# Attention and soft mixture of experts: x turned by transposing transfers, one exponential tile in every step on VectorE

## Chip, cores, metric

One core of a Trainium2 chip. The metric is the device time of one execution in microseconds (us). Most executions of a kernel agree within 0.3%; a run 1.5% above the fastest of its kernel counts as slow and is left out of ratios.

## The reference

```python
# q, k, v: (8, 12, 448, 64); phi: (768, 32); w1: (8, 768, 1024); w2: (8, 1024, 768)
scores = cap * np.tanh((q @ k.T) / 8 / cap)            # cap = 30
attn = softmax(scores); x = (attn @ v)                 # -> x: (3584, 768)
logits = x @ phi
d = softmax over tokens of logits; slot_input = d.T @ x
slot_out = relu(slot_input @ w1) @ w2                  # per expert
out = softmax over slots of logits @ slot_out
```

The attention output x is needed twice: as it is, for `slot_input`, and with its columns on the partitions, for `logits`. Turning x is what the change is about.

## The kernel before

The loop has 56 steps, seven to a batch of 12 heads (six pairs). In a step ScalarE takes the tanh and the exponential of six tiles of 448 columns. `aux` holds side jobs by step and slot; a step runs its slots in the order "a", "b", the rest of the product with V with its norm, "c", "d". In these traces each engine starts its instructions in program order.

One tile of a step can be taken by VectorE, as five operations, here in five of seven steps:

```python
    PARTS = {0: ((0, "a", (0, 1)), (0, "d", (2, 3)), (1, "a", (4,))),
             ...                       # the same for 1, 2, 3 and 6
    def poly_exp(j, ops):
        t = exs[j][:, 0, :]
        steps = (
            lambda: dve.tensor_scalar(xe, t, ...),                        # to an integer
            lambda: dve.tensor_scalar(xb.bitcast(U16), whole, 7, None, ALU.logical_shift_left),
            lambda: dve.scalar_tensor_tensor(xp, frac, p2, frac, ALU.add, ALU.mult),
            lambda: dve.scalar_tensor_tensor(xp, xp, p1, frac, ALU.add, ALU.mult),
            lambda: dve.scalar_tensor_tensor(t, xp, p0, xb, ALU.add, ALU.mult))
```

The norm, the turning of x and the logits:

```python
    def norm(pr, s0, s1, pv):
        ...
        dve.reciprocal(rec, pv[:, 0:s1 - s0, DH:W])
        dve.tensor_tensor(xq[Q][:, h, s0:s1, :], pv[:, 0:s1 - s0, 0:DH], rec..., op=ALU.mult)

    def x_transp(pr):
        ps = psT.tile([P, S], BF16, name="xps", tag="T")      # tag "T": one PSUM buffer
        turn_x(ps, 0, pr, range(NG))                          # TensorE transposes
        t = xs.tile([P, S], BF16, name="xT", tag="xT", bufs=2)
        dve.tensor_copy(t, ps)
        xTs[pr] = t

    def logits(Q, ps=None):
        ps = psT.tile([P, NG, NS], F32, name="lps", tag="T")
        ...                                                   # matmuls phib x xT, two pairs
        dve.tensor_copy(lgs[b], ps)                           # or an add
```

The loads of q, k and of all weights cast from f32 and are issued by GpSimd (the software queue); v comes plain, issued by SP. GpSimd also casts v.

The softmax here doesn't subtract the row's maximum and nothing guards it: scores larger than these inputs give would overflow.

## Time and profile before

| | before |
|---|---|
| time | 311.0 us (median of four) |
| span of the profiled run, mean clock of TensorE | 312.0 us, 0.987 |
| a batch, by the distance of norms | 31.6 us |
| landing of v / q / k, median | 5.1 / 8.4 / 6.9 us |

### The profile page before, as it was taken

The page shows a single profiled execution, that of the slowest core. Times are in us where ns is not written, and L with a number is a line of the kernel's source. Part 1 is how long each engine was busy: PE and PEld are TensorE (multiplying, and loading weights), DVE is VectorE, ACT ScalarE, POOL GpSimd, SP SyncE. Part 2 cuts the span into 40 slices and gives each one's busy share as a digit, 9 for nine tenths or more (in the row PEclk, how much of TensorE's full clock was granted, in tenths as well). Part 3 has the DMA queues.
Part 4 walks back from the last instruction along what each step waited for, and adds up shares of the span by engine and source line. Part 5 has one row for each costly group of instructions (what it writes and reads, how often), then busy time and mean ns, then how long its engine had stood idle before and what let it go on. Part 6 is the DMA issues. An engine that isn't in the chain of part 4 may idle for free.

```text
span 312.0 us, 11360 instructions
## 1 busy us (share of the span) xinstructions
PE 272.0 (87%) x5069; PEld 191.5 (61%) x5069; DVE 212.9 (68%) x463; ACT 271.9 (87%) x209; POOL 135.8 (44%) x176
## 2 busy tenths in 40 slices
PE   8999889998999988988899889888998899998820
PEld 6666666676667766666676667666766677642400
DVE  2533589958995899589958995799578944236840
ACT  3899999999999999999999999999999997126730
POOL 4192836393639345924492549155913350000000
PEclk9999999999999999999999999999999999999995
DMA  7979999999999999999899999999999548948997
GB/s 262 188 140 204 196 185 181 205 192 200 208 218 185 192 219 200 204 202 223 157 178 211 207 217 182 195 220 223 179 204 205 115 159 313 352 155 298 391 410 313
DMA packets 57488, 67.75 MB, mean 217 GB/s; under 512 B 3808, under 2 KB 53600, under 8 KB 57440
## 3 DMA queue, kind: packets, MB, share of 16 engines
q0 software_dynamic: 42448, 35.31, 73.6%
q1 hardware_dynamic: 14704, 31.50, 29.4%
q8 instruction: 39, 0.64, 0.8%
q10 hardware_dynamic: 288, 0.23, 0.2%
q14 instruction: 9, 0.07, 0.1%
HBM read 91.32 MB, written 18.87 MB: 353 GB/s over the span
## 4 chain that ended last, share of the span: by engine, by line
PE 46%; DVE 40%; ACT 8%; issue 2%; DMA 1%; DVEq 0%; ACTq 0%
PE pv L353 11%; DVE xq L361 7%; PE sc L295 7%; PE junk L595 6%; DVE work L333 5%; DVE work L334 5%; DVE ex L335 5%; DVE work L332 4%; ACT ex L304 3%; ACT ex L308 3%; DVE work L330 3%; DVE kT L265 3%; DVE qT L265 2%; DVE xT L410 2%; PE kps L263 2%; PE pv L381 2%
## 5 line engine op out<-in xcount | busy, mean ns | idle before, releaser
L304 ACT ACTIVATE ex<-sc 128x1344 bf16<-128x1344 f32 (+1 forms) x113 | 152.1, 1510 | 3.8 <-PE sc L295 3.7
L308 ACT ACTIVATE ex<-ex 128x2240 bf16<-128x2240 bf16 (+4 forms) x58 | 137.1, 2368 | 0.1
L353 PE MATMUL pv<-vbd,ex 128*128 128x130 bf16 (+1 forms) x1610 | 94.3, 211 | 13.8 <-DVE xq L361 11.5
L353 PEld LDWEIGHTS <-ex 128*128 128x128 bf16 (+1 forms) x1680 | 75.9, 101 | 34.2 <-DVE xq L361 9.6
L295 PE MATMUL sc<-qT,kT 64*64 64x448 bf16 x672 | 74.0, 364 | 2.2 <-DVE qT L265 1.3
L273 POOL CAST vbd<-vraw 64x896 bf16<-64x896 f32 x23 | 21.4, 929 | 83.6 <-PE pv L353 73.5
L447 POOL COPY e<-E 128x512 bf16<-128x512 bf16 x9 | 6.4, 715 | 64.9 <-ACT E L441 30.8
L410 DVE COPY xT<-xps 128x448 bf16<-128x448 bf16 x47 | 18.2, 388 | 23.8 <-PE xps L404 23.4
L361 DVE TENSOR_TENSOR xq<-pv,rec 128x448 bf16<-128x448 f32 x46 | 28.7, 624 | 1.6
L295 PEld LDWEIGHTS <-kT 64*64 64x64 bf16 x672 | 24.9, 106 | 7.0 <-issue 4.9
L333 DVE SCALAR_TENSOR_TENSOR work<-work 128x448 f32<-128x448 uint16 x35 | 26.6, 761 | 0.0
L595 PEld LDWEIGHTS <-ones 128*128 128x128 bf16 x326 | 20.5, 105 | 8.1 <-issue 5.2
L334 DVE SCALAR_TENSOR_TENSOR work<-work 128x448 f32<-128x448 f32 x35 | 24.4, 697 | 1.2
L110 POOL DMA_DIRECT2D w1b<-in_moe_w_dram x32 | 24.7, 773 | 0.0
L274 POOL CAST vbd<-vraw 64x896 bf16<-64x896 f32 x23 | 23.3, 1014 | 1.4
L381 PE MATMUL pv<-ones 128*128 128x57 bf16 x620 | 23.9, 188 | 0.0
L595 PE MATMUL junk<-ones 128*128 128x128 bf16 x283 | 21.5, 225 | 1.2 <-DVE xq L361 1.0
L335 DVE SCALAR_TENSOR_TENSOR ex<-work 128x448 bf16<-128x448 f32 x35 | 21.9, 626 | 0.2
L265 DVE COPY kT<-kps 128x896 bf16<-128x896 bf16 x23 | 14.3, 621 | 11.1 <-PE kps L263 9.7
L381 PEld LDWEIGHTS <-ones 128*128 128x128 bf16 x620 | 20.7, 96 | 0.3
L265 DVE COPY qT<-qps 128x896 bf16<-128x896 bf16 x23 | 14.2, 618 | 5.8 <-PE qps L263 5.8
L182 POOL DMA_DIRECT2D qb<-in_q_dram x22 | 16.4, 745 | 3.8 <-DMA kraw<-in_k_dram 3.8
(117 smaller groups left out, 343.1 us busy)
## 6 DMA issues: line engine op xcount, KB each, us to landing
w1b<-in_moe_w_dram POOLq DMA_DIRECT2D x32, 384.0 KB, 8.7
vraw<-in_v_dram SPq DMA_DIRECT2D x23, 448.0 KB, 5.1
w2d<-in_moe_w_dram POOLq DMA_DIRECT2D x20, 384.0 KB, 8.6
w2t<-w2d SPq DMA_DIRECT2D x20, 384.0 KB, 5.7
out_dram<-ob SPq DMA_DIRECT2D x8, 768.0 KB, 6.8
qb<-in_q_dram POOLq DMA_DIRECT2D x22, 224.0 KB, 8.4
kb<-in_k_dram POOLq DMA_DIRECT2D x22, 224.0 KB, 6.9
w2b<-in_moe_w_dram POOLq DMA_DIRECT2D x12, 384.0 KB, 8.3
```

Source lines behind the costliest of these rows:

```text
L110: pool.dma_start(out=w1b[e][:, js, fs], in_=w1r[:, e, js, fs])
L265: dve.tensor_copy(t, ps)
L295: pe.matmul(sc[cs, u, 0:S], qkT["k", Q][r, c, cs], qkT["q", Q][r, :, cs], start=True, stop=True)
L304: act.activation(exs[j][:, half * CS + u0:half * CS + u1, :], sc[:, u0:u1, 0:S], ACT.Tanh, scale=qk_scale / cap)
L308: act.activation(exs[j][:, u0:u1, :], exs[j][:, u0:u1, :], ACT.Exp, scale=cap)
L333: lambda: dve.scalar_tensor_tensor(xp, frac, p2, frac, ALU.add, ALU.mult),
L334: lambda: dve.scalar_tensor_tensor(xp, xp, p1, frac, ALU.add, ALU.mult),
L335: lambda: dve.scalar_tensor_tensor(t, xp, p0, xb, ALU.add, ALU.mult))
L353: pe.matmul(out_, exs[j][r, u, q0:q0 + (HP if tail else P)], v_, start=(c == 0 and g == gs[0] < NF), stop=(c == NT - 1), skip_group_check= ...
L361: dve.tensor_tensor(xq[Q][:, h, s0:s1, :], pv[:, 0:s1 - s0, 0:DH], rec.to_broadcast([P, s1 - s0, DH]), op=ALU.mult)
L381: pe.matmul(home, ones, ones[:, 0:512 - NT * W], start=False, stop=True, skip_group_check=True)
L595: pe.matmul(junk if home is None else home, ones, ones, start=True, stop=True)
```

## The change

Its intent: free TensorE of turning x and VectorE of copying the turned x, by letting a transposing transfer do it, and use the time that VectorE gets to take an exponential tile in all seven steps. The five operations of a tile are spread over the step so that no norm or copy waits long. x moves into one long buffer `xall` of eight slots; its column groups are reordered so that one transfer of 128 x 512 serves a pair; the odd group of 64 is covered by two small matmuls with `phi2`.

```diff
-    PARTS = {0: ((0, "a", (0, 1)), (0, "d", (2, 3)), (1, "a", (4,))),  ... 1, 2, 3, 6 alike
+    PARTS = {0: ((0, "<b", (0,)), (0, "c", (1, 2, 3)), (0, ">d", (4,))),
+             1: ((0, "a", (0,)), (0, "r", (1,)), (0, "c", (2, 3)), (0, ">d", (4,))),
+             ...
+             5: ((0, "<d", (0,)), (1, "<b", (1,)), (1, ">b", (2,)), (1, "c", (3,)), (1, ">d", (4,))),
+             6: ((0, "a", (0,)), (0, ">b", (1,)), (0, ">d", (2,)), (1, "<b", (3, 4)))}
@@ norm: slot "r" lies between the reciprocal and the multiplication
+        for f, a in between:
+            f(*a)
@@ x_transp
+        if pr < NDX:                                   # all but the last four pairs
+            x0 = pr % 8 * S
+            t = xs.tile([P, NG, P], BF16, name="xT", tag="xT", bufs=3)
+            sp.dma_start_transpose(out=t, in_=xall[:, x0:x0 + HP + S])
+            xTs[pr] = t
+            return
@@ phi_mms, the tail of 64
+            for m in range(2):
+                for n, ph in enumerate((phi2, phib)):
+                    pe.matmul(dst[m * HP:m * HP + HP], t[HP:P, 0, n * HP:n * HP + HP], ...)
@@ fillers (dependence-free matmuls): 106 per batch before, 82 after; places of the jobs
-            at(j + 4 + k, "a", x_transp, p + k)
+            at(*((j + 3 + k, "c") if p + k < NDX else (j + 4 + k, "a")), x_transp, p + k)
... (cut: start of the kernel, tile sizes, the end part's slots)
```

## The prediction

> **What bounds the kernel now.** The work up to about 257 us is a loop of 56 steps: ScalarE (ACT) takes two tanh of 1344 columns and one exponential of 2688 columns per step, TensorE (PE) makes scores and the product with V, VectorE (DVE) copies, norms, and in five of each seven steps takes one 448-column tile of the exponential as a polynomial of five instructions. Seven steps are one batch.
>
> I read the chain of work that ended last first, from the page:
>
> ```profile
> PE 46%; DVE 40%; ACT 8%; issue 2%; DMA 1%; DVEq 0%; ACTq 0%
> ```
>
> ACT is 8% of it, though the page has ACT at nine tenths or more in the slices of the loop. The stretches by engine, of two batches in the middle, say how full each engine is:
>
> ```profile
> 99.30:130.93 31.63, 28.93 (x592) 21.09 (x591) 25.38 (x56) 31.63 (x24) 18.63 (x23) 1.00 1.16 202
> 130.93:162.59 31.66, 28.50 (x584) 20.78 (x585) 25.67 (x55) 31.66 (x24) 17.00 (x23) 1.00 1.12 185
> ```
>
> (Columns: length, PE, PE weight load, DVE, ACT, POOL, clock, DMA share, GB/s.) A batch takes 31.63 us; ACT has no idle time, PE 2.7 us, DVE 6.25 us. The timeline of ACT tells the two apart, by the starts:
>
> ```profile
> 98.38 2.76 ACT L304 ACTIVATE ex<-sc 128x1344 bf16<-128x1344 f32 x2
> ...
> 103.05 2.78 ACT L304 ACTIVATE ex<-sc 128x1344 bf16<-128x1344 f32 x2
> ...
> 107.35 2.80 ACT L304 ACTIVATE ex<-sc 128x1344 bf16<-128x1344 f32 x2
> ...
> 129.42 2.89 ACT L304 ACTIVATE ex<-sc 128x1344 bf16<-128x1344 f32 x2
> ```
>
> A step in which ACT does all six tiles is 103.05 - 98.38 = 4.67 us, one in which DVE takes a tile 107.35 - 103.05 = 4.30 us, so a tile is worth 0.37 us. Seven steps of ACT are 5 x 4.30 + 2 x 4.67 + 0.20 (a small exponential) = 31.04 us, just 129.42 - 98.38. But the loop of PE and DVE needs 31.63 us: the norm, in the chain in order of time,
>
> ```profile
> 106.96 0.62 DVE xq L361
> ...
> 111.29 0.64 DVE xq L361
> ...
> 138.59 0.62 DVE xq L361
> ```
>
> comes again after 138.59 - 106.96 = 31.63 us. So PE, which starts with a lead, loses about 0.6 us of it to ACT per batch, and late in the loop ACT waits:
>
> ```profile
> 241.27 1.30 ACT L304 ACTIVATE ex<-sc 128x1344 bf16<-128x1344 f32 x1
> 242.98 1.29 ACT L304 ACTIVATE ex<-sc 128x1344 bf16<-128x1344 f32 x1 [0.41 <-PE sc L295]
> ```
>
> 1.71 us between these two starts instead of the usual 1.17 (a pair without a wait takes 2.34, as from 98.38 to 100.72 us). All such excess of the starts from 170 us on I sum to about 2.0 us. So **ACT and the PE-DVE loop bind together**, 31.04 and 31.63 us per batch. Inside the loop DVE has no idle between 103.07 and 123.7 us (the five steps with a polynomial); in the other two steps PE has none, filler matmuls included.
>
> The third thing is DMA, from the DMA view of the same batch (99.3 to 131 us):
>
> ```profile
> q0 software_dynamic: 5259, 4.94, 100.5%
> q1 hardware_dynamic: 823, 1.39, 14.5%
> ```
>
> The casting loads write 4.94 MB and, being f32 at the source, read 9.88 MB; with v's 1.39 MB that is 11.3 MB in 31.63 us, 356 GB/s. The best slice of the page is 410 GB/s, so the engines are about 87% full.
>
> **What the Trainium skill says.** "DMA: Bandwidth & Descriptors", section "DMA Transpose (X-bar)": the plain transposing transfer is issued from SP or ACT, takes 2-byte types and writes SBUF; only two such streams at once are unsafe. Here all go from SP. No transfer of this trace transposes, so its speed isn't shown. The same page, "Anatomy of one DMA", puts about 2.0 us of fixed time on a transfer on the software path; the trace agrees for the hardware path too in that the smallest stores (192 KB) land in a median of 2.1 us. Its section "Issuing engines are not separate DMA queues" has all queues on the same 16 engines: the trace agrees, v's 448 KB take 5.1 us beside the software queue. "VectorE: DVE Perf Modes", "The three transpose paths", gives 1309 ns for a 128x128 by DMA against 390 ns on PE; here PE records 219 ns each, three pipelined in 0.33 us.
>
> **The change part by part, per batch.**
>
> ACT: two more tiles go to DVE, 31.04 - 2 x 0.37 = 30.3 us. In the whole loop 48 tiles instead of 35: 13 x 0.37 = 4.8 us less.
>
> DVE loses six copies of x (L410) and gains two polynomials. The groups give their means:
>
> ```profile
> L410 DVE COPY xT<-xps 128x448 bf16<-128x448 bf16 x47 | 18.2, 388 | 23.8 <-PE xps L404 23.4
> ...
> L333 DVE SCALAR_TENSOR_TENSOR work<-work 128x448 f32<-128x448 uint16 x35 | 26.6, 761 | 0.0
> ...
> L334 DVE SCALAR_TENSOR_TENSOR work<-work 128x448 f32<-128x448 f32 x35 | 24.4, 697 | 1.2
> ```
>
> A polynomial is 398 + 421 + 761 + 697 + 626 = 2903 ns by the means, about 2.6 us by the distance of starts where nothing disturbs it. A copy is 0.39 us, 0.31 by starts. So 25.4 + 2 x 2.75 - 6 x 0.33 = 28.9 us. Part of the mean is a disturbance: an L334 at 108.27 takes 1.25 us instead of 0.62 while POOL casts v. With a polynomial in every step all three casts of a batch can meet one, say 0.3 us more: **29.2 us of 30.3, 96%**. That is why the operations are spread, one even between the reciprocal and the multiplication.
>
> PE loses six times three 128-wide and two 64-wide transposes, about 0.42 us each set as they issue (108.84 to 109.15 us and the matmuls they hold up), 2.4 us; gains six times two small matmuls for the tail, some 0.3 us; and the fillers go from 106 to 82, about 1 us. 28.9 - 3.1 = 25.8 us: it no longer binds in any step, and the wait of DVE for the transposes (23.4 us in the whole run) goes.
>
> DMA: six transposes of 128 x 512 x 2 B = 131 KB, 0.79 MB. Then (11.3 + 0.79) MB in 30.3 us = 399 GB/s, **97% of the best slice**, if a transpose moves as fast as a copy. Each has from the end of its norm to the logits of its pair: now 107.6 to 111.0 us, 3.4 us, at the shortest. Estimate for landing: between the 2.1 us of the smallest store and v's 5.1 us, some 3 us, since it has less than a third of v's bytes. It hides, with little to spare; PE can wait another microsecond, as the scores are that far ahead of ACT.
>
> Start and end: three pairs of fillers fall out of the first transposes, at most 0.3 us. The last four pairs keep the old way, so from 257 us all shifts as it is.
>
> The sum, if ACT alone binds: 4.8 us of tiles + 2.0 us of late waits + 0.1 = 6.9 us, 311.0 - 6.9 = 304.1 us. I don't expect all of it. DVE at 96%, in order, will wait here and there for PE, and what it waits it can't get back. If DVE and PE turn at 30.8 us per batch instead of 30.3, that is 7 x 0.5 = 3.5 us, of which the lead PE starts with hides about 1.5: 2.0 us lost, **306 us**.
>
> **The rivals.** First, *DVE becomes the bound*: for it speak the 96% and the full DVE between 103 and 124 us; against it that DVE's long waits were for the x transposes that go, and that the order was plainly arranged with care. At 31.2 us per batch: 7 x 0.9 - 1.5 = 4.8 lost, 309 us. Second, *DMA becomes the bound or lands late*: for it the 97% and a transpose slower than a copy; against it that the weights leave some slack outside full batches. With transposes at half the speed of a copy the demand is 12.9 MB, 31.4 us at 410 GB/s, late q or k loads would stall PE, 309 to 311 us; if each logits waited 1.5 us more for a transpose, 3 x 7 x 1.5 us, even a third of it kept gives over 315. Third, *ACT keeps the pace*: 304 us. For it the three microseconds that PE gets per batch.
>
> **Range and chances.** ACT's pace 35% (304), a partly lost pace 45% (about 306.5), DVE or DMA as the bound 16% (309 to 311), late transposes 4% (over 315). 2% faster is under 304.7, which only the first can give, and not all of its cases. Predicted 306.0 us, range 303.5 to 310.0; faster 0.27, same 0.69, slower 0.04.
>
> **What would show it.** In the profile after: starts of ACT 4.30 us apart in all steps; the batch by the norm (now 31.63 us) at 30.3 to 31.0; DVE in a middle batch 28.5 to 29.5 us busy; PE some 26; x transposes landing in about 3 us, with no wait of PE for them of weight; DMA share higher; the part after the loop unchanged within 0.5 us. A median landing over 5 us, waits of the logits' matmuls for the transfers, DVE without idle time with ACT waiting for scores, or a loop that ends no earlier would make the prediction wrong.

## More of the kernel before

The lines that carry the argument stand in the prediction. A few more are wanted for comparison. The page's clock row, one digit per fortieth of the span, in tenths of full speed:

```profile
PEclk9999999999999999999999999999999999999995
```

and from the list of waits (engine, line, what it waited for: us in total, times, longest), the only wait of ScalarE in the loop:

```profile
ACT ex L304 <- PE sc L295: 3.7, 5, 2.0
```

The clock is at 90% or more until the last slice, and ScalarE nearly never waits for scores. The DMA view's issues have the two landing times from which the prediction estimates that of a transpose, v's and the smallest store's, and between them q's (KB each, median us from issue to landing):

```profile
vraw<-in_v_dram SPq DMA_DIRECT2D x23, 448.0 KB, 5.1
...
qb<-in_q_dram POOLq DMA_DIRECT2D x22, 224.0 KB, 8.4
...
out_dram<-obh SPq DMA_DIRECT2D x20, 192.0 KB, 2.1
```

## The result

| | before | after |
|---|---|---|
| time, median (lowest to highest) | 311.0 us | 363.1 us (360.3 to 367.7) |
| ratio after/before | | 1.164, 95% interval 1.155 to 1.173 |
| span, mean clock | 312.0 us, 0.987 | 360.0 us, 0.893 |
| time at half clock inside the loop | 0 | 68 us |
| from the norm of pair 45 of 48 to the end | 51.8 us | 52.45 us |
| landing of v / q / k, median | 5.1 / 8.4 / 6.9 us | 6.5 / 9.5 / 7.1 us |

The time at half clock is counted up to the norm of pair 45; the texts below say 61 us, which leaves out its last stretch, 6.8 us from 282.7 us on. A ratio is the mean time of one kernel's fast runs over the mean of the other's in the same rounds, so it isn't quite the ratio of the medians in the table. The change is slower by 16%. All of it lies in the loop. The page's chain of work that ended last, by engine and then by line, now reads:

```profile
PE 41%; DMA 27%; DVE 23%; ACT 4%; issue 2%; DVEq 0%; SPq 0%; ACTq 0%
DMA xT<-xall 25%; PE pv L360 14%; PE sc L300 6%; DVE xall L369 5%; PE kps L260 4%; DVE work L340 3%; DVE work L341 3%; DVE work L339 3%; PE junk L621 2%; DVE ex L342 2%; DVE work L337 2%; ACT ex L309 2%; PE so_ps L794 2%; PE pv L388 2%; PE hp L766 2%
```

DMA was 1% of this chain and is 27%; 25% are the transposing transfers alone. The tile view of the turned x has their time from issue to landing, and the list of waits has who paid:

```profile
DMA to landing us min/median/max: 2.4/7.0/11.8
```

```profile
PEld L430 <- DMA xT<-xall: 44.1, 21, 5.5
ACT ex L309 <- PE sc L300: 42.5, 30, 5.7
PE lps L430 <- DMA xT<-xall: 37.7, 16, 5.4
```

L430 are the logits. The profile keeps weight loads (PEld) and matmuls (PE) of TensorE on two tracks, and both wait for the same transfers here, so 44.1 and 37.7 us are largely the same time and are not added. TensorE stands, the next scores come late, and ScalarE, which waited 3.7 us before, waits 42.5 us. One such wait, in the chain in order of time (start, length, what):

```profile
115.52 0.64 DVE xall L369
116.21 8.01 DMA xT<-xall
124.27 0.32 PE lps L430 x5
...
138.54 0.54 DVE xall L369
139.13 7.04 DMA xT<-xall
```

and the same place in the timeline of TensorE, where the bracket is the idle time before:

```profile
116.30 0.85 PE L360 MATMUL pv<-vbd,ex 128*128 128x130 bf16 x12 [0.23 <-DVE xall L369]
...
124.27 0.32 PE L430 MATMUL lps<-phib,xT 128*128 128x32 bf16 x5 [4.89 <-DMA xT<-xall]
...
124.84 1.50 PE L360 MATMUL pv<-vbd,ex 128*128 128x130 bf16 x12
```

The norm ends at 116.2 us; the transfer lands 8 us later; TensorE stands 4.89 us of these. The same twelve matmuls then take 1.50 instead of 0.85 us, because the clock has been halved (granted clock 0.50 from 124.84 to 126.34 us). The page's clock row shows how often that happens:

```profile
PEclk9999888998999789688885997996999799999995
```

What the change was for does come where nothing disturbs it. The timeline of ScalarE:

```profile
101.10 2.45 ACT L309 ACTIVATE ex<-sc 128x1344 bf16<-128x1344 f32 x2
...
105.40 2.48 ACT L309 ACTIVATE ex<-sc 128x1344 bf16<-128x1344 f32 x2
...
127.58 1.29 ACT L309 ACTIVATE ex<-sc 128x1344 bf16<-128x1344 f32 x1 [4.17 <-PE sc L300]
```

4.30 us from step to step at first, then 4.17 us of waiting. The stretches by engine, of two middle batches (length, PE, weight load, DVE, ACT, POOL, clock, DMA share, GB/s):

```profile
104.46:142.00 37.54, 28.80 (x547) 20.95 (x547) 29.33 (x61) 30.89 (x23) 17.84 (x23) 0.91 1.29 187
142.00:180.00 38.00, 31.84 (x510) 22.49 (x509) 27.55 (x58) 30.61 (x23) 16.43 (x22) 0.78 1.14 180
```

No engine is full: 37.5 us for 30.9 us of ScalarE.

A side finding, about the result and not the time. The timeline of VectorE shows the first operation of two tiles (L337) before the second operation (L339) of either:

```profile
106.92 0.38 DVE L337 TENSOR_SCALAR work<-ex 128x448 int32<-128x448 bf16 x1
...
108.45 0.38 DVE L337 TENSOR_SCALAR work<-ex 128x448 int32<-128x448 bf16 x1
108.86 0.43 DVE L339 TENSOR_SCALAR work<-work 128x448 uint16<-128x448 uint16 x1
```

In `PARTS`, residue 5 starts its tile in slot "<d" and goes on in the next step's "<b", after residue 6 has overwritten the shared `work` in "a". By the code and by the order in this trace that tile gets its neighbour's exponential. The comparison with the reference passes all the same, as it does when x isn't turned at all (run 6), so it is blind to both. The kernel after is thus not right as it stands, nor is any run below with these places; it is an error to mend in any use of them.

### The profile page after: what moved, and what is told of

Its sections match the earlier page's. It is cut to its first block, busy times and chain, and to the rows that moved or that the text cites.

```text
span 360.0 us, 10935 instructions
## 1 busy us (share of the span) xinstructions
PE 280.0 (78%) x4764; PEld 196.2 (55%) x4764; DVE 234.2 (65%) x484; ACT 270.6 (75%) x209; POOL 136.7 (38%) x178
## 4 chain that ended last, share of the span: by engine, by line
PE 41%; DMA 27%; DVE 23%; ACT 4%; issue 2%; DVEq 0%; SPq 0%; ACTq 0%
DMA xT<-xall 25%; PE pv L360 14%; PE sc L300 6%; DVE xall L369 5%; PE kps L260 4%; DVE work L340 3%; DVE work L341 3%; DVE work L339 3%; PE junk L621 2%; DVE ex L342 2%; DVE work L337 2%; ACT ex L309 2%; PE so_ps L794 2%; PE pv L388 2%; PE hp L766 2%
## 5 line engine op out<-in xcount | busy, mean ns | idle before, releaser
L309 ACT ACTIVATE ex<-sc 128x1344 bf16<-128x1344 f32 (+1 forms) x113 | 141.0, 1289 | 42.7 <-PE sc L300 42.5
L313 ACT ACTIVATE ex<-ex 128x2240 bf16<-128x2240 bf16 (+4 forms) x58 | 119.6, 2066 | 0.1
L360 PE MATMUL pv<-vbd,ex 128*128 128x130 bf16 (+1 forms) x1610 | 105.5, 225 | 11.4 <-DVE xall L369 7.5
L360 PEld LDWEIGHTS <-ex 128*128 128x128 bf16 (+1 forms) x1680 | 84.9, 108 | 34.4 <-issue 9.1
L430 PE MATMUL lps<-phib,xT 128*128 128x32 bf16 x132 | 9.6, 183 | 42.0 <-DMA xT<-xall 37.7
L340 DVE SCALAR_TENSOR_TENSOR work<-work 128x448 f32<-128x448 uint16 x48 | 36.9, 769 | 0.2
L262 DVE COPY kT<-kps 128x896 bf16<-128x896 bf16 x23 | 14.3, 624 | 31.1 <-PE kps L260 30.9
L430 PEld LDWEIGHTS <-xT 128*128 128x128 bf16 x132 | 6.2, 99 | 49.6 <-DMA xT<-xall 44.1
L341 DVE SCALAR_TENSOR_TENSOR work<-work 128x448 f32<-128x448 f32 x48 | 31.8, 663 | 1.4
L342 DVE SCALAR_TENSOR_TENSOR ex<-work 128x448 bf16<-128x448 f32 x48 | 29.7, 618 | 0.4
L369 DVE TENSOR_TENSOR xall<-pv,rec 128x448 bf16<-128x448 f32 x46 | 28.5, 619 | 1.1
L339 DVE TENSOR_SCALAR work<-work 128x448 uint16<-128x448 uint16 x48 | 26.4, 550 | 0.5
L388 PEld LDWEIGHTS <-ones 128*128 128x128 bf16 x506 | 20.6, 103 | 0.0
```

The source lines that it names most:

```text
L309: act.activation(exs[j][:, half * CS + u0:half * CS + u1, :], sc[:, u0:u1, 0:S], ACT.Tanh, scale=qk_scale / cap)
L313: act.activation(exs[j][:, u0:u1, :], exs[j][:, u0:u1, :], ACT.Exp, scale=cap)
L360: pe.matmul(out_, exs[j][r, u, q0:q0 + (HP if tail else P)], v_, start=(c == 0 and g == gs[0] < NF), stop=(c == NT - 1), skip_group_check= ...
L369: dve.tensor_tensor(xq[pr][:, s0:s1, :], pv[:, 0:s1 - s0, 0:DH], rec.to_broadcast([P, s1 - s0, DH]), op=ALU.mult)
L388: pe.matmul(home, ones, ones[:, 0:512 - NT * W], start=False, stop=True, skip_group_check=True)
```

## The experiments

Theory L (landing): the transposes land too late and TensorE waits for them in the logits. Rivals: the spread of VectorE's operations holds TensorE up (S); the transposes' traffic holds up the loads of q, k and v (T); the halved clock is a cost of its own (C). "Wrong" means that the logits get an x that isn't turned.

**1. Turning on TensorE again**, the rest as after.

```diff
-    NDX = NPAIR - 4
+    NDX = 0
```

> The changed kernel, but x is turned on TensorE and copied by VectorE again, as in the kernel before; VectorE keeps a tile of the exponential in every step. Theory (the transposing transfers alone cost the time, by landing in 7 us where 3.4 us are free): no wait for xT is left and the time falls from 363 to 303 to 312 us, with the granted clock back at 0.98. Rival (the spread of the five operations holds VectorE and TensorE up): over 330 us.

340.3 us, ratio 1.095 [1.090, 1.100]: 23 of the 53 us come back, 30 remain. That is the outcome that the text gave to the rival S, not to theory L. But VectorE now has copies and seven polynomials, so this run alone doesn't decide; runs 2, 6 and 11 to 13 do. From the waits, and from its timeline one disturbed operation in slot "r":

```profile
ACT ex L309 <- PE sc L300: 24.5, 36, 1.7
DVE xT L423 <- PE xps L410: 20.0, 29, 1.7
PE xps L405 <- DVE lg L459: 7.2, 12, 0.7
```

```profile
166.93 1.86 DVE L339 TENSOR_SCALAR work<-work 128x448 uint16<-128x448 uint16 x1
```

Many short waits, round in a circle between VectorE and TensorE. So seven tiles at these places leave no room for turning on TensorE; the loss of this run is not the loss of the change.

**2. The old five places of the tile**, with the transfers (`PARTS` as before).

> The changed kernel with the transposing transfers, but VectorE takes its tile in five steps of seven in the three pieces of the kernel before. Theory (transfers): 355 to 370 us, TensorE waiting some 80 us for xT as in the changed kernel. Rival (spread of the operations): under 335 us.

One fast run of 359.0 us and three slow, 366.2 to 368.9, so no ratio; the fast runs of after took 360.3 to 364.5 us. It is hardly better than after. S falls as the cause of the loss: with VectorE relieved, the transfers give nearly all of it.

**3. A plain copy of the same bytes in place of each transpose** (wrong).

```diff
-            sp.dma_start_transpose(out=t, in_=xall[:, x0:x0 + HP + S])
+            sp.dma_start(out=t.rearrange("p g q -> p (g q)"), in_=xall[:, x0:x0 + HP + S])
```

> The changed kernel with a plain copy of the same 128 x 512 bf16 in place of each transposing transfer, on the same queue at the same place (wrong result on purpose). If any transfer on that queue comes late because it shares the engines with the casting loads: landings stay at a median of 6 to 7 us and the time over 340 us. If it is the transposing itself: landings of 3 to 4 us, waits for xT under 15 us, and a time of 303 to 315 us.

333.1 us, ratio 1.070; landing 5.6 us in the median. Even a plain copy doesn't land in 3 us here, and the logits wait for it (20.7 us on the weight loads' track, in a profiled run, slow). That lies between the two outcomes of the text. With copies 23 of the 53 us of the loss are there.

**4. The weights' loads moved to the loop's end** (one look; its total is meaningless, only the loop is read).

```diff
-        at(1 + n * (NCH - 5) // len(wjobs), "b", *job)
+        at(NCH - 2, "b", *job)
```

> The changed kernel with all weight loads issued at the end of the loop (its whole time is not to be compared; the loop is). If sharing the engines with the casting loads makes the transposing transfers late: landings mostly 2.4 to 4 us in the loop, waits for xT under 15 us, and batches by the norm 4 to 5 us shorter than in the changed kernel (38.6 us). If they are late by themselves: nothing changes.

The transposes land in 4.2 us instead of 7.0, the norm of pair 45 comes at 273.4 us instead of 307.5. The waits for x fall from 44.1 to 20.8 us on the weight loads' track, not under 15 us as the text asked. The company of other loads makes the landing late.

**5. One transfer at a time beside three kinds of loads** (a kernel of its own, one look, output wrong on purpose): four transposes or copies of 128 x 512, each waiting for the one before, alone and beside ten loads that read 786 KB each.

> Landing by itself (wrong result on purpose): four transfers of 128 x 512 bf16, one after the other, transposing and then plain, first with nothing beside them, then beside ten loads of 768 KB each: casting f32 to bf16 on the software queue, not casting on the software queue, not casting on ScalarE's queue. If the transposing transfer suffers from small packets that take turns with any other queue's, all three backgrounds give 5 us and more for it. If only casting loads do it, the other two give under 4 us. Alone I expect 2.5 us transposing and 2 us plain; plain beside loads 3 to 4 us.

Its chain in order of time has, in this order, a copy alone, a transpose alone, a copy beside casting loads, and a transpose beside loads that don't cast:

```profile
33.84 1.95 DMA t<-x
...
41.77 2.40 DMA t<-x
...
56.31 5.45 DMA t<-x
...
74.50 11.47 DMA t<-x
```

Alone 2.4 against 1.95 to 2.06 us; beside casting loads 6.1 to 7.9 against 5.5 to 6.9; beside plain loads in the software queue 10.5 to 11.5 against 6.5 to 7.8; beside plain loads in ScalarE's queue 5.8 to 8.7 against 5.7 to 6.6. (The last one or two of each four, with most loads over, are left out: 2.4 to 4.7 us.) The text had expected 3 to 4 us for a copy beside loads. The ten casting loads themselves took as long beside transposes as beside copies (22.5 and 22.3 us from the first packet to the last). So 7 us is the ordinary landing time in this company; the loads of a later stage here had started early, so the stages are not all as they were meant.

**6. No turning at all**: the logits read `xall` itself (wrong). Meant as the most that the change could give.

```diff
-            t = xs.tile(...); sp.dma_start_transpose(out=t, in_=...); xTs[pr] = t
+            xTs[pr] = xall[:, x0:x0 + HP + S].rearrange("p (g q) -> p g q", q=P)
```

> The changed kernel, but x is not turned at all: the logits read x itself where they read the turned tile (wrong result on purpose), so nothing lands late, no extra bytes move, and TensorE and VectorE have no work in its place. This is the most that the change can give. If late landings are the whole loss: 303 to 309 us, ScalarE back to back. If the five spread operations also cost (the run that turned x on TensorE took 340 us): 318 to 335 us, with the batch by the norm at 33 us or more.

310.2 us, ratio 0.998 [0.994, 1.001]: nothing. With x turned for free, seven tiles on VectorE give no gain. Summed by the excess of its starts over their usual distances, from 24 us to the end of the loop, ScalarE loses 6.4 us here against 2.0 us before: 4.4 us more, most of the 4.8 us that the tiles save it. One place where that begins: VectorE's shift in slot "r" takes 1.30 us (GpSimd issues loads and begins a cast of v in that time; whether that is the cause wasn't tested), the multiplication follows late, and TensorE waits for it. The timelines of VectorE and of TensorE:

```profile
121.36 1.30 DVE L339 TENSOR_SCALAR work<-work 128x448 uint16<-128x448 uint16 x1
122.59 0.60 DVE L369 TENSOR_TENSOR xall<-pv,rec 128x448 bf16<-128x448 f32 x1
```

```profile
123.34 0.85 PE L360 MATMUL pv<-vbd,ex 128*128 128x130 bf16 x12 [0.95 <-DVE xall L369]
```

**7. No turning, and the old five places.**

> The same without any turning of x, but with VectorE's tile in five steps of seven and in the old three pieces. If the spread is what costs beside the landings: 304 to 311 us, clearly below the run without turning that has the spread. If the fillers, taken down from 106 to 82 per batch, or the new layout of x cost instead: it stays above 318 us too.

308.6 us, ratio 0.994 [0.992, 0.996]. With five tiles it is no slower than with seven. Free turning with either set of places lies within 1% of the kernel before. Other places were not tried with it.

**8. The logits two steps later**, so that a transfer has some 8 us more (nine slots in `xall`, five turned tiles, and to make room four fewer w2 blocks kept on chip).

> The changed kernel with the logits and all that follows from them two steps later, so that a transposing transfer has about 12 us instead of 3.4 (five tiles for turned x instead of three, nine slots instead of eight, and four weight blocks fewer kept on chip to make room). If the landing's latency is what costs: the waits for xT fall from 82 to under 10 us and the time to that of the run without turning, within 6 us. If the transfers cost by holding up the other loads: xT waits vanish, but TensorE waits for k and q and the time stays above 345 us.

338.6 us, ratio 1.091, between the two outcomes of the text. The wait of the logits is gone (1.6 us on the weight loads' track), and yet only 24 of 53 us come back. The wait has moved to v:

```profile
POOL vbd L270 <- DMA vraw<-in_v_dram: 48.3, 7, 8.3
ACT ex L309 <- PE sc L300: 27.3, 19, 3.6
```

The part from the norm of pair 45 on is as long as in after (52.5 us), so the four w2 blocks don't explain the rest. L alone can't be the whole loss; T gets weight here.

**9. A hundred fillers ahead of each logits**, to keep TensorE and its clock up while it waits.

```diff
+        at(j + 5, "d", fill, 100)        # and ahead of the other two logits
```

> The changed kernel with 100 small filler matmuls (about 3.3 us at 33 ns) ahead of each logits, where TensorE waits 3.7 us on average for the turned x. Theory (the waits cost twice, because the clock is halved for 3.41 us and more after them; 61 us of the loop ran at half clock): TensorE is blocked as long as before, but the slow time falls under 30 us and the run from 363 to 335 to 350 us. Rival (the clock costs nothing, since TensorE waits anyway): within 2% of the changed kernel, or slower by the fillers.

382.9 us, ratio 1.233, against the 335 to 350 us of the theory. Half clock shrinks from 68 to 3.4 us and the waits for transposes vanish, but the fillers' matmuls grow from 23 to 85 us, more than the 38 to 44 us of waiting they replace, and wait themselves for the norm that frees their PSUM buffer (15.7 us).

**10. Forty-five fillers** at the same places:

> The kernel after with 45 fillers instead of 100 ahead of each logits, some 1.5 us of work in place of part of the wait of PE (mean 3.7 us). If the halved clock is a cost of its own, the fillers shorten the half-clock stretches (61 us) to under 40 us and the time falls below 363 to 345 to 355 us. If the wait is the loss and the clock only follows it, 358 to 370 us.

366.5 us (one fast run of 359.3, three slow around 367, so no ratio), inside the 358 to 370 us of "the clock only follows". Half clock 34 us, waits for the transposes halved (21.2 us), fillers 51 us. The mean wait of 3.7 us in that text had added two tracks; it is about 2. Neither run isolates C. What can be said is a bound: in the half-clock stretches of after, TensorE's matmuls were busy 61 us (first one of the start included), so halving can have cost them at most 31 us; how much of that lies on the path stays open.

**11 to 13. Around run 1.** The operation of slot "r" moved behind the multiplication; the logits' evacuation by VectorE put ahead of the polynomial ("<d" to "d" in `PARTS`), both with turning on TensorE; and the kernel before with one line changed, its old places in all seven steps:

> The run that turned x on TensorE (340 us), with the one operation that stands between the reciprocal and the multiplication of the norm put after the multiplication. If this operation, which took up to 1.86 us beside GpSimd's cast in place of 0.39 and held the norm up, is a large part of the 30 us: 325 to 332 us. If not: over 335 us.

> The run that turned x on TensorE (340 us), with VectorE's operations that stood ahead of its evacuation of the logits put behind it. TensorE turns the next x in the same PSUM bank and waits for that evacuation. If this order is a large part of the 30 us: 322 to 332 us. If not: over 335 us.

> The kernel before with one line changed: VectorE takes a tile in all seven steps, in the three old pieces at the old places. If the number of tiles is what overloads VectorE (25.4 + 5.5 = 30.9 us of a 31.6 us batch): 315 to 330 us. If only the new places of the five operations cost: 305 to 312 us.

344.9 us (1.111), 325.5 us (1.049) and 323.2 us (1.043). The place of the shift isn't the cause of run 1's loss. The order is a part of it: the logits sit in the only PSUM buffer "T", and while VectorE does two operations of a tile first, TensorE can't write the next transposes; 15 us come from that. And without the transfers, seven tiles fill VectorE by plain sums, 25.4 + 2 x 2.75 = 30.9 of 31.6 us, and the run at the old places is 13 us slower.

**14 and 15. Transposes issued, but unread; copies issued, but unread** (wrong): the transfers as in after or in run 3, while the logits read `xall`. Nobody waits for a landing, only the traffic is left.

```diff
-            xTs[pr] = t
+            xTs[pr] = xall[:, x0:x0 + HP + S].rearrange("p (g q) -> p g q", q=P)
```

> The kernel after, with all its 44 transposing transfers issued as they are, but the logits read x itself and so never wait for a landing (wrong on purpose, within the tolerance, as the run without any turning was). It parts the cost of the transposes' traffic from the cost of waiting for them. Theory A, the wait for the landing is the loss and the traffic costs little: 310 to 316 us, as without any turning (310.2), half clock under 12 us. Theory B, the traffic alone holds up the loads of q, k and v: 320 to 340 us, with waits of PE for qb and kb or of POOL for vraw of over 10 us, as the run with the logits two steps later had (338.6). I hold the two at 50 to 50.

> The same with a plain copy of the same bytes in place of each transposing transfer, unread as well. If the transposing form holds up the loads more than its bytes do, this comes out below the unread transposes by over 4 us, near 310 to 314; if bytes alone count, the two are within 2 us of each other.

332.2 us (1.071) and 308.0 us (0.993). These two part the loss (medians of all four runs, the slow too, beside a kernel before at 310 to 311 us):

| us | logits read x itself | logits wait for the transfer |
|---|---|---|
| no transfer | 310.2 | |
| plain copy | 308.0 | 333.1 |
| transpose | 332.2 | 363.1 |

Down the first column: the bytes cost nothing, the transposing form costs 24 us though nobody reads its result. (Why unread copies come out 2 us below no transfer at all wasn't asked.) Across: waiting for the landing costs 25 us for a copy and 31 us for a transpose. Both L and T hold, about half each. The clock isn't parted from either: half clock in the loop was 3.4 us in run 15, 41 us in run 14, 48 us in run 3 (its profile is slow) and 68 us in after. The pages' queue rows (packets, MB, share of 16 engines' span) of the unread transposes and of the unread copies:

```profile
q0 software_dynamic: 42848, 35.34, 72.9%
q1 hardware_dynamic: 38640, 37.27, 44.7%
```

```profile
q0 software_dynamic: 42848, 35.34, 73.9%
q1 hardware_dynamic: 21040, 37.27, 35.6%
```

The same bytes, in 17,600 packets more: 400 for each of 44 transposes: in these traces a transpose moves as 512 packets of 256 bytes, a copy as 128 of 1024. As times of all 16 engines, 44.7% of 329.5 us against 35.6% of 305.9 us is 147.3 against 108.9 us, 0.87 us more per transpose; and the packets of the casting queue took 240.2 against 226.1 us for the same work. q's loads land in 12.4 against 9.4 us, k's in 10.8 against 7.8, v's in 8.1 against 6.5. GpSimd's wait for v, in the two kernels:

```profile
POOL vbd L270 <- DMA vraw<-in_v_dram: 47.5, 12, 7.2
```

```profile
POOL vbd L270 <- DMA vraw<-in_v_dram: 15.8, 6, 4.7
```

**16. Twelve in a row** (a kernel of its own, one look, output zeros): transposes and copies alone, and beside eight casting loads of 384 KB, without and with v's loads in the transposes' queue.

> A kernel of its own (wrong on purpose: the output is zeros): eight stages, one after the other, each begun by VectorE and ended by its reads of all that landed. 1: twelve transposing transfers of 128 x 512 bf16 in a row, nothing else; 2: twelve plain copies of the same bytes; 3: eight casting loads of 384 KB alone; 4: these with the twelve transposes; 5: these with the twelve copies; 6 to 8: as 3 to 5 with four plain loads of 448 KB on the transposes' own queue, one after each three. It asks why unread transposes cost 24 us more than unread copies. Theory A, a transpose takes more of the 16 engines than its bytes: some 1 to 1.5 us each in stage 1 against 0.4 to 0.6 in stage 2, and stage 4 longer than stage 5 by 6 us or more. Theory B, it only lands late and holds up what stands behind it in its own queue: stages 4 and 5 within 2 us, but the loads of stage 7 land later than those of stage 8 by some us.

VectorE reads one column of each as it lands. Its timeline, two landings of transposes alone, then two of copies alone:

```profile
9.32 0.15 DVE L102 CAST z<-t 128x1 f32<-128x1 bf16 x1 [1.14 <-DMA t<-x]
10.60 0.15 DVE L102 CAST z<-t 128x1 f32<-128x1 bf16 x1 [1.12 <-DMA t<-x]
...
25.26 0.15 DVE L102 CAST z<-t 128x1 f32<-128x1 bf16 x1 [0.48 <-DMA t<-x]
25.97 0.15 DVE L102 CAST z<-t 128x1 f32<-128x1 bf16 x1 [0.55 <-DMA t<-x]
```

and from the tile view, what issuing costs on SP's queue (ns, min/median/max):

```profile
L95 SPq DMA_TRANSPOSE t<-x x36: 1191/1274/5861, 1.4 to 157.2; - x36
L97 SPq DMA_DIRECT2D t<-x x36: 465/599/1409, 19.3 to 178.3; - x36
```

A transpose every 1.3 us, a copy every 0.64 us; the issue alone takes 1.19 us. The stages, from mark to mark: loads alone 20.2 us, with transposes 29.9, with copies 25.2; with v's loads 24.3, 35.9 and 32.1. Theory A had asked for 6 us between transposes and copies and got 4.7 and 3.8: the sign is right, the size smaller. But the casting loads' last packet came 21.3 us after their first beside transposes and 22.1 beside copies, so here they were not held up more; v's last load landed 34 us into its stage against 28 us with copies. That spoke for B, so

**17. v out of SP's queue**: run 14 with v's loads issued by GpSimd.

```diff
-            (sp if nm == "v" else pool).dma_start(out=t, in_=quad_ap(nm, Q))
+            pool.dma_start(out=t, in_=quad_ap(nm, Q))
```

> The run with the transposes issued but unread (332.2 us), with v's loads issued by GpSimd right behind v's casts, as plain loads in the software queue, instead of by SP between the transposes. Theory B, the transposes hold up v because both are issued in order by SP, and late v holds up GpSimd, which casts v and issues the loads of q and k: below 318 us, with waits of POOL for vraw under 20 us (47.5 in the run before it). Theory A, the transposes slow the loads whatever their queue: 325 to 340 us, qb landing still at 11 us or more. A time in between, or a higher one with vraw landing over 10 us, settles nothing, since v then stands behind q, k and the weights.

344.0 us, ratio 1.110, q landing 11.7 us, GpSimd's wait for v 39.9 us. That is over both ranges of the text (A's ended at 340 us), with v landing in 8.3 us, so the move itself costs something, and no unread copies were run with v there. But there is no gain, and q is as late as A asked: B falls as the main cause. The loads land late in the software queue too. How a transpose holds them up on the 16 engines, which the microbenchmark with its single source doesn't reproduce, stays open.

**18. A candidate**: the kernel before with a sixth tile (residue 4).

> A candidate to beat both: the kernel before with VectorE taking a tile in six of the seven steps (the one with residue 4 added), nothing else changed. ACT gives up 8 tiles of the 13 x 0.37 us; VectorE goes from 25.4 to some 28.1 us of 31.6. With seven of seven it was 323 us. I expect 309 to 316 us: the copies of x stand in the steps without a polynomial, and one of these is lost. Below 308 if ACT's pace is what counts.

315.1 us, ratio 1.015 [1.013, 1.018]: 1.5% slower, clear of noise. No run found a correct version that beats the kernel before.

## Why the prediction was wrong

- **The landing, the step that failed.** "Estimate for landing: between the 2.1 us of the smallest store and v's 5.1 us, some 3 us, since it has less than a third of v's bytes. It hides, with little to spare". Measured: 7.0 us. The smallest store was taken from the end of the kernel, where no load runs beside it. In the loop q's 224 KB took 8.4 us, so landing time did not follow bytes; that row stood in the profile of before (the page's DMA issues) and wasn't used. Runs 3 and 5 show the same for copies (5.6 us; 5.5 to 6.9 us beside casting loads). Waiting costs 25 to 31 us (run 3 against 15, after against 14).
- **DMA as bytes per second.** "(11.3 + 0.79) MB in 30.3 us = 399 GB/s, 97% of the best slice, if a transpose moves as fast as a copy." The bytes were no problem: unread copies of them ran at 308.0 us. Its own view had the packets of the casting queue at 100.5% of the 16 engines' span, which by that count leaves no engine free; judged by bytes this became 87% full. And the condition was false: 24 us for the transposing form (run 14 against 15). The second rival named this ("a transpose slower than a copy") but sized it at 309 to 311 us, by its bytes doubled, and not by its packets or by what late loads stop.
- **The weight of the rival.** "late transposes 4% (over 315)": the mechanism that came was in the list, "if each logits waited 1.5 us more", and the wait was right in kind: some 2 us per logits (44.1 us over 21 waits). What was underrated is its chance, with 3.4 us of room and an estimate from two numbers that both came from other conditions.
- **The clock.** Not in the prediction at all. The kernel before is filled with dependence-free matmuls, and its loop has no half clock. With 24 fillers per batch less and no wait for transfers (runs 6, 7 and 15) it was 3.4 to 6.8 us; with the transfers and their waits 68 us, at most 31 us of matmul time, its share of the path not settled.
- **ScalarE's gain.** "31.04 - 2 x 0.37 = 30.3 us" and steps of 4.30 us: right where nothing waits (101.10 to 105.40). "VectorE at 96%, in order, will wait here and there" was right in kind and too small: with turning for free the time is 310.2 us (run 6), not 306, and ScalarE loses 4.4 us more than before. That the waits between VectorE and TensorE are behind all of it is read from one place, not tested. The readings under it were too strong: "no idle between 103.07 and 123.7 us" is 19.8 us busy of 20.6 for VectorE, and TensorE, said to have none in the other two steps, was busy 10.8 of 12.0 us.
- **VectorE's load.** 29.2 us predicted, 29.3 and 27.6 us measured in the two middle batches, which are 38 us long instead of 30.3: right as work. **TensorE's**: 25.8 us predicted; 26.7 us at full clock in run 15 (stretch 103.9 to 135.7 us). **The part after the loop**: unchanged within 0.5 us predicted, 0.65 us longer measured.
- **What would show it wrong.** The list had "a median landing over 5 us, waits of the logits' matmuls for the transfers": both are there.

## What to carry to other kernels

Estimate the landing time of a new transfer from the slowest small transfer that runs in the same stretch of the kernel, not from bytes and not from an idle stretch, and put it against the time to its first reader before anything else. To part what a transfer costs, issue it and leave it unread, and do the same with a plain copy of its bytes: three runs tell bytes, form and wait apart. And before an engine is relieved at a price, run the kernel with the relief for free: here that run said that, with these places, there was nothing to gain.

## What the Trainium skill lacked or had wrong

- "Advanced Engine Details and Errata", section "X-Bar Transpose (TRN2)": it has transposing transfers as fast as regular ones, about 90% of a copy's bandwidth. Twelve of 131 KB in a row took 1.3 us each against 0.64 us for copies, about half, with 1.19 us for the issue on SP alone, so the rate of the transfer itself isn't shown; alone 2.4 against 1.95 to 2.06 us; beside plain loads in the software queue 10.5 to 11.5 against 6.5 to 7.8 us.
- "DMA: Bandwidth & Descriptors", section "DMA Transpose (X-bar)": nothing there on the cost of issuing (1.19 us on SP against 0.46 us for a copy, up to 5.9 us beside loads) or on what a transpose does to other queues' loads (q's landing 9.4 to 12.4 us, 24 us of the kernel's time).
- The same page, section "Anatomy of one DMA", written for the software path: a fixed 2.0 us and bytes. Alone it holds for SP's transfers too (copies of 131 KB in 1.95 to 2.06 us), not beside loaded queues, where the same copy took 5.5 to 6.9 us; we found no page with a figure for that.
- "VectorE: DVE Perf Modes", section "The three transpose paths": 1309 ns for a 128 x 128 by transfer. Here a 128 x 512 lands in 2.4 us alone and in 7.0 us (median) in the kernel; the page doesn't say that the figure is for an idle chip.
- "TensorE: Matmul & The Clock Gate", section "Why this matters for your kernels": no idle gaps over some 3 us. In run 15 half clock, for 3.41 us, followed an idle stretch of 1.20 us (at 33.1 us), while one of 1.36 us (at 123.5 us) had no such effect; the length of a single gap doesn't decide it.
